# Attention and an MLP mixer on one core: order settings by 32 score tiles, a second buffer for the MLP's inner layer, and a last inversion between block transposes

## The chip, the core and the metric

One Trainium2 chip, one core. The metric is the device time of one execution in microseconds.

## The reference

A gate mixes a 32-head attention block with a shifting MLP; all inputs are bf16, S = 2048, D = 512, F = 1792.

```python
def _A_ref(x, wqkv, wo):                       # 32 heads of 16
    q, k, v = split_heads(x @ wqkv)
    p = softmax(einsum("bhqd,bhkd->bhqk", q, k) * 16 ** -0.5)
    return merge_heads(einsum("bhqk,bhkd->bhqd", p, v)) @ wo

def _B_ref(x, w1, w2, w3, w4):
    h = gelu(layernorm(x) @ w1)
    hs = shift_quarters_along_S(h) @ w2        # by +1, -1, +2, -2
    x1 = x + hs
    return x1 + gelu(layernorm(x1) @ w3) @ w4  # w3: 512x1792

g = sigmoid((x * gate_w).sum(-1, keepdims=True))
return g * _A_ref(x, ...) + (1 - g) * _B_ref(x, ...)
```

## The kernel before

The attention is done in 32 rounds (4 chunks of 512 queries, 4 groups of 8 heads, 2 halves). A round has 64 score tiles: 4 heads, each with 16 blocks of 128 keys against 512 queries. In all there are 2048 tiles. TensorE makes scores in its row mode (contraction over 32 rows, four heads one below the other) and everything else, the products with V ("PV") and all projections, in its column mode. A tile's exponential goes one of two ways:

- ScalarE takes two tiles in one 1024-wide exponential (buffers PA).
- VectorE takes one tile by a trick on the bits of the number, then adds three constant shifts to a pair of tiles (buffers PD). Two shifts run on VectorE, the third usually on GpSimd. All four versions are multiplied by V and summed on TensorE.

What makes this kernel unusual is that the order of its instructions comes from a list scheduler inside the kernel. It carries a duration for each operation, plays the engines forward when the kernel is built, and emits the instructions in the order in which they started. I call what it computes the plan. Its constants decide what TensorE takes next:

```python
    DVE_STOP = 6        # VectorE takes no more tiles when so few are left in a round
    AHEAD = 9           # how early the next round may begin
    FILL = 250          # how long TensorE idles before it multiplies zeros
    SL = (45, 60)       # slack in the budget of column work
    # ... some twenty more, one value each for the whole kernel
    P_W3 = ((740, 900), (975, 1250), (1314, 1520), (1719, 1830))   # first layer of the inner MLP, by tile
    P_W4 = ((991, 903), (1260, 1330), (1560, 1640), (1850, 2008))  # second layer
    NPA, NPD, NW = 9, 16, 9                                         # buffers
    # ...
    def pe_pick():
        # 1. new scores for ScalarE and VectorE wherever a PSUM bank is free
        # ...
        # 2. otherwise column work, as much as fits until the next bank comes free
        tr = min((j.start + j.hold + j.lat for j in exps if ...), default=None)
        budget = tr - t + SL[turn[0]] if tr is not None else IDLE_NS
        n = min(int(budget // 216.0), MAXU)
        g = gen_ready()                # a projection or an MLP product that is due
        # ... do_gen() and do_pv() in an order set by the constants
        if not ops:
            return filler(tr)          # matmuls of zeros
```

The GpSimd shift, the one inner-layer buffer and the product at the end of a round:

```python
    # close_pair, third shift of a pair of VectorE tiles (w = 1024):
    nc.gpsimd.tensor_scalar(out=d[k][:, 0:w], in0=d[0 if both else 2][:, 0:w], scalar1=1.0,
                            scalar2=float(SHIFT * (k if both else 1)), op0=ALU.mult, op1=ALU.add)
    # ... mlp2: all four chunks use hT
    h2 = hT[:].rearrange("p k s -> p (k s)")[:, 0:FT * 512].rearrange("p (f t) -> p f t", f=FT)
    # ... finish_round
    n = gp(1250, d3, lambda: nc.gpsimd.tensor_tensor(out=ob.slot[:], in0=ab.slot[:], in1=bb.slot[:], op=ALU.mult), ...)
```

The end of the kernel, where the last round's sums are inverted through TensorE:

```python
    nc.scalar.copy(out=ab[:], in_=acc[:])
    known(2); known(3)                                  # products that don't need the last round
    for b in range(4):                                  # the sums come onto partitions
        nc.tensor.matmul(pd[:, 4 * b:4 * b + 4], lhsT=ab[:, b * P:(b + 1) * P], rhs=idf[:, 0:P:32], ...)
    add_y(1)
    nc.vector.reciprocal(out=rdl[:], in_=pd.rearrange("p (b j) -> p b j", j=4))
    nc.vector.tensor_tensor(out=rdl[:], in0=rdl[:], in1=zE[...], op=ALU.mult)
    for b in range(4):                                  # and are spread again
        for j in range(4):
            nc.tensor.matmul(bc[32 * j:32 * j + 32, b * P:(b + 1) * P], lhsT=rdl[:, b, j:j + 1].to_broadcast([P, 32]), ...)
    add_y(3)
    for h in range(2):
        nc.vector.tensor_tensor(out=oT[...], in0=ab[...], in1=bc[...], op=ALU.mult)
```

The softmax here doesn't subtract the row's maximum and nothing guards it: scores larger than these inputs give would overflow.

## Time and profile before

| | before |
|---|---|
| median of 3 runs (lowest to highest) | 794.11 us (792.35 to 794.57) |
| span of the profiled execution | 790.1 us |
| PE, DVE, ACT busy | 98%, 95%, 94% |
| exponentials on ScalarE, tiles on VectorE | 736, 577 |
| matmuls of zeros | 300 |

Most lines are shown in the prediction. This is the timeline of TensorE in the kernel before: start in us, length in us, engine and line, operation, output and inputs, shapes, count.

```profile
7.50 1.05 PE L506 MATMUL ring<-w,w 128*32 128x512 bf16 x16
8.37 1.04 PE L506 MATMUL ring<-w,wq 128*32 128x512 bf16 x16
...
10.64 0.40 PE L812 MATMUL psA<-q,kT 32*128 32x512 bf16 x4
```

The first K projection runs at 7.50, and the first scores at 10.64.

A ledger of ScalarE is the measure used below. From the starts of all exponentials in the trace:

span = first exponential + pairs of neighbours x 0.903 us + what the pairs lose beyond 0.903 + other work (the GELUs) + from the last exponential to the end.

For the kernel before it reads 11.1 + 658.3 (729 pairs) + 57.9 + 51.0 + 11.8 = 790.1 us. The 57.9 is the room the change is after.

### The profile page before, as it was taken

The page shows a single profiled execution, that of the slowest core. Times are in us where ns is not written, and L with a number is a line of the kernel's source. Part 1 is how long each engine was busy: PE and PEld are TensorE (multiplying, and loading weights), DVE is VectorE, ACT ScalarE, POOL GpSimd, SP SyncE. Part 2 cuts the span into 40 slices and gives each one's busy share as a digit, 9 for nine tenths or more (in the row PEclk, how much of TensorE's full clock was granted, in tenths as well). Part 3 has the DMA queues.
Part 4 walks back from the last instruction along what each step waited for, and adds up shares of the span by engine and source line. Part 5 has one row for each costly group of instructions (what it writes and reads, how often), then busy time and mean ns, then how long its engine had stood idle before and what let it go on. Part 6 is the DMA issues. An engine that isn't in the chain of part 4 may idle for free.

```text
span 790.1 us, 24272 instructions
## 1 busy us (share of the span) xinstructions
PE 771.3 (98%) x9849; PEld 232.9 (29%) x9849; DVE 749.7 (95%) x1598; ACT 740.2 (94%) x762; POOL 343.8 (44%) x337
## 2 busy tenths in 40 slices
PE   8999999999899999999999999999999999999997
PEld 4333332222322222233222223222223222222223
DVE  6999999999999999999989999899999999999985
ACT  6999999999999999999989999999999999999995
POOL 3334343545444444453444434444444444444541
PEclk9999999999999999999999999999999999999999
DMA  9321302231000112143100011011000000000001
GB/s 210 116 57 54 80 7 73 44 92 66 20 3 20 51 39 57 33 114 104 30 24 22 20 26 39 29 27 37 22 19 19 23 27 29 11 20 19 17 19 32
DMA packets 64984, 34.63 MB, mean 44 GB/s; under 512 B 44636, under 2 KB 60268, under 8 KB 64872
## 3 DMA queue, kind: packets, MB, share of 16 engines
q1 hardware_dynamic: 63400, 32.42, 16.0%
q8 instruction: 77, 1.26, 0.7%
q10 hardware_dynamic: 1472, 0.66, 0.3%
q14 instruction: 35, 0.29, 0.1%
HBM read 17.39 MB, written 6.81 MB: 31 GB/s over the span
## 4 chain that ended last, share of the span: by engine, by line
PE 64%; DVE 26%; ACT 4%; issue 3%; DMA 1%; SPq 0%; POOL 0%; DVEq 0%; POOLq 0%; ACTq 0%
PE acc L988 22%; PE ring L506 20%; PE psA L812 20%; DVE PD L918 11%; DVE PD L954 8%; ACT PA L892 3%; DVE st L645 1%; PE ring L812 1%; DVE xn L665 1%; DVE hT L735 1%; DVE x_sb L714 1%; ACT hT L736 1%; DMA x_sb<-in_A_x_dram 1%; DVE accsb L1004 1%; DVE q L577 0%
## 5 line engine op out<-in xcount | busy, mean ns | idle before, releaser
L892 ACT ACTIVATE PA<-psA 128x1024 bf16<-128x1024 f32 x736 | 689.5, 1039 | 35.4 <-PE psA L812 18.4
L957 POOL TENSOR_SCALAR PD<-PD 128x1024 uint16<-128x1024 uint16 x275 | 289.4, 1053 | 412.1 <-DVE PD L954 291.2
L918 DVE TENSOR_SCALAR PD<-ring 128x512 uint16<-128x512 f32 x577 | 376.5, 679 | 12.4 <-PE ring L812 10.8
L988 PE MATMUL acc<-PD,V 128*17 128x512 bf16 x2308 | 308.9, 381 | 3.1 <-DVE PD L954 2.5
L812 PE MATMUL psA<-q,kT 32*128 32x512 bf16 x1471 | 279.1, 384 | 1.2 <-ACT PA L892 0.9
L988 PE MATMUL acc<-PA,V 128*17 128x512 bf16 x1471 | 268.3, 381 | 1.7 <-DVE accsb L1004 1.7
L954 DVE TENSOR_SCALAR PD<-PD 128x1024 uint16<-128x1024 uint16 (+1 forms) x592 | 240.9, 448 | 2.7
L812 PE MATMUL ring<-q,kT 32*128 32x512 bf16 x577 | 188.8, 383 | 1.3 <-DVE PD L918 1.2
L812 PEld LDWEIGHTS <-kT 32*128 32x128 bf16 x2048 | 72.6, 91 | 299.0 <-issue 298.1
L988 PEld LDWEIGHTS <-V 128*17 128x17 bf16 x3779 | 78.3, 88 | 142.1 <-issue 117.6
L506 PE MATMUL ring<-xnT,w 128*32 128x512 bf16 x1152 | 95.1, 383 | 2.3 <-DVE PD L918 2.2
L506 PE MATMUL ring<-w,hT 128*32 128x512 bf16 x1152 | 92.8, 383 | 1.8 <-DVE PD L918 0.8
L506 PEld LDWEIGHTS <-w 128*32 128x32 bf16 x1920 | 43.8, 95 | 49.8 <-issue 37.0
L1021 POOL TENSOR_TENSOR oT<-accsb,bcs 128x512 bf16<-128x512 f32 x31 | 40.4, 1305 | 8.5 <-DMA bcs<-rr 7.2
L506 PE MATMUL ring<-w,w 128*32 128x256 bf16 (+1 forms) x768 | 40.8, 311 | 0.5 <-DVE PD L918 0.4
L735 DVE CAST hT<-ring 128x512 bf16<-128x512 f32 x56 | 37.8, 678 | 0.9 <-PE ring L506 0.8
L506 PEld LDWEIGHTS <-hT 128*32 128x32 bf16 x1152 | 25.1, 95 | 36.0 <-issue 27.3
L1004 DVE COPY accsb<-acc 128x512 f32<-128x512 f32 x31 | 21.1, 681 | 4.7 <-PE acc L988 4.1
L736 ACT ACTIVATE hT<-hT 128x7168 bf16<-128x7168 bf16 x4 | 24.7, 6178 | 0.0
L645 DVE BATCH_NORM_STATS2 st<-x_sb 128x6 f32<-128x512 bf16 x32 | 21.6, 679 | 0.0
L1242 PE MATMUL acc<-zero 128*17 128x384 bf16 x300 | 20.6, 327 | 0.0
L506 PE MATMUL ring<-w,wq 128*32 128x512 bf16 x256 | 19.9, 382 | 0.0
(92 smaller groups left out, 233.8 us busy)
## 6 DMA issues: line engine op xcount, KB each, us to landing
bcs<-rr SPq DMA_DIRECT2D x124, 64.0 KB
xn_dram<-xn SPq DMA_DIRECT2D x32, 128.0 KB
w<-in_B_w_dram SPq DMA_DIRECT2D x5, 512.0 KB
oD<-oT SPq DMA_DIRECT2D x124, 16.0 KB
w<-in_B_w_dram SPq DMA_DIRECT2D x4, 448.0 KB
out_dram<-ot SPq DMA_DIRECT2D x14, 128.0 KB
x_sb<-in_A_x_dram SPq DMA_DIRECT2D x3, 512.0 KB
w<-in_A_wqkv_dram SPq DMA_DIRECT2D x2, 256.0 KB
```

The lines of the kernel that those rows point to most:

```text
L506: units.append([Op("col", j, lambda j=j, lf=lf, rf=rf, n0=n0, n1=n1, st=st, sp=sp: nc.tensor.matmul(get()[32 * j:32 * j + 32, n0:n1], lhsT ...
L645: a = dve(600, deps, lambda: nc.vector.bn_stats(out=sb.slot[:], in_=x_sb[:, t, :]), prio=6, at=at, acq=[sb])
L735: pre.append(evac(g, PSUM_NS, lambda ps, m=m: nc.vector.tensor_copy(out=h2[:, m, :], in_=ps[:])))
L736: ge = act(93 + 427 * FT + 2600, pre, lambda: nc.scalar.activation(out=h2, in_=h2, func=ACT.Gelu_apprx_tanh), prio=0)
L812: o = Op("row", i, lambda: nc.tensor.matmul(dst(), lhsT=kT[G][32 * i:32 * i + 32, kt * P:(kt + 1) * P], rhs=qbuf[G, c].slot[32 * i:32 * i ...
L892: job = act(hold, ops, lambda: nc.scalar.activation(out=pb.slot[:, 0:n], in_=buf.slot[:, 0:n], func=ACT.Exp, scale=0.25), acq=[pb], frees= ...
L918: nc.vector.tensor_scalar(out=pr["buf"].slot[:, h * 512:(h + 1) * 512], in0=buf.slot[:], scalar1=BITS_MUL, scalar2=BITS_ADD, op0=ALU.mult, ...
L954: nc.vector.tensor_scalar(out=d[k][:, 0:w], in0=d[0][:, 0:w], scalar1=float(SHIFT * k), scalar2=None, op0=ALU.add)
L957: nc.gpsimd.tensor_scalar(out=d[k][:, 0:w], in0=d[0 if both else 2][:, 0:w], scalar1=1.0, scalar2=float(SHIFT * (k if both else 1)), op0=A ...
L988: o = Op("col", i, lambda: nc.tensor.matmul(acc[32 * i:32 * i + DH + 1, :], lhsT=lhs(), rhs=rhs(), start=st, stop=True, tile_position=(0, ...
L1004: e = dve(PSUM_NS, round_ops[r], lambda: nc.vector.tensor_copy(out=ab.slot[:], in_=acc[:]), acq=[ab], prio=0)
L1021: n = gp(1250, d3, lambda: nc.gpsimd.tensor_tensor(out=ob.slot[:], in0=ab.slot[:], in1=bb.slot[:], op=ALU.mult), acq=[ob], frees=[ab, bb], ...
```

## The change

Its intent: give each stretch of 32 score tiles its own settings of the order; let two chunks of the inner layer overlap; invert the last round on VectorE alone. The core of the diff, with cuts marked:

```diff
-    DVE_STOP = 6
-    AHEAD = 9
-    ... (and some twenty more constants)
-    P_W3 = (..., (1719, 1830))
-    P_W4 = (..., (1560, 1640), (1850, 2008))
+    P_W3 = (..., (1525, 1830))
+    P_W4 = (..., (1560, 1715), (1850, 2008))
+    T1_DUE = 8
+    BASE = dict(P1_PRIO=0.414, DVE_STOP=6, DVE_STOP_L=8, AHEAD=9, IDLE_NS=537, ...)
+    SEG = 32
+    STAGES = {0: {'DUE_SH': -20, 'AHEAD': 7, 'GP2': 0.35}, 2: {'S_PRIO': 0.324}, ... , 64: {...}}
+    K = SimpleNamespace(**BASE)
-    NPA, NPD, NW = 9, 16, 9
+    NPA, NPD, NW = 8, 12, 9
+    hB = const.tile([P, FT * 512], BF16, name="hB")
+    h_of = {0: hT[...][:, 0:FT * 512], 1: hB[:]}
-        "xn": slots("xn", 4, [P, D]),
+        "xn": slots("xn", 2, [P, D]),
-        "big": [hT],
+        "big": [0, 1],
-        "bcs": slots("bcs", 2, [P, 512], F32),
+        "bcs": slots("bcs", 1, [P, 512], F32),
 ... first x transposes: blocks paired 0 and 2, 1 and 3
-        ks = (2 * half, 2 * half + 1)
+        ks = (half, half + 2)
 ... first Q projection (the first K projection keeps due=-3)
-                ... due=at + QDUE - QAT if at >= 0 else -1)
+                ... due=at + QDUE - QAT if at >= 0 else -4)
 ... pe_pick
+        if sim.tiles // SEG != stage[0]:
+            stage[0] = sim.tiles // SEG
+            K.__dict__.update({**BASE, **STAGES.get(stage[0], {})})
 ... the end
-    nc.scalar.copy(out=ab[:], in_=acc[:])
-    ... the two sets of matmuls through TensorE
+    nc.vector.transpose(out=tr[0][:], in_=acc[:])
+    nc.vector.reciprocal(out=rdl[:], in_=by32(tr[0])[:, :, 0])
+    nc.vector.tensor_tensor(out=rdl[:], in0=rdl[:], in1=zL[:], op=ALU.mult)
+    nc.vector.transpose(out=by32(tr[1]), in_=rdl[:].unsqueeze(2).to_broadcast([P, NT, 32]))
```

## The prediction

> **What bounds the kernel now.** I read the page's totals first, then the chain, the groups, the waits of ScalarE, and last the timeline at three places.
>
> ```profile
> span 790.1 us, 24272 instructions
> PE 771.3 (98%) x9849; PEld 232.9 (29%) x9849; DVE 749.7 (95%) x1598; ACT 740.2 (94%) x762; POOL 343.8 (44%) x337
> ...
> PE 64%; DVE 26%; ACT 4%; issue 3%; DMA 1%; SPq 0%; POOL 0%; DVEq 0%; POOLq 0%; ACTq 0%
> ...
> L892 ACT ACTIVATE PA<-psA 128x1024 bf16<-128x1024 f32 x736 | 689.5, 1039 | 35.4 <-PE psA L812 18.4
> L957 POOL TENSOR_SCALAR PD<-PD 128x1024 uint16<-128x1024 uint16 x275 | 289.4, 1053 | 412.1 <-DVE PD L954 291.2
> L918 DVE TENSOR_SCALAR PD<-ring 128x512 uint16<-128x512 f32 x577 | 376.5, 679 | 12.4 <-PE ring L812 10.8
> ...
> L1242 PE MATMUL acc<-zero 128*17 128x384 bf16 x300 | 20.6, 327 | 0.0
> ```
>
> Three engines are loaded nearly alike, and the chain hops between them: no single one is "the" bound. Busy time flatters them (a busy PE may be draining, a busy DVE may be held by GpSimd), so I counted in the trace records what each needs at its own shortest pace.
> - ScalarE: neighbouring exponentials start at best 0.903 us apart. 736 of them and the five GELUs with their table loads need about 714 us.
> - VectorE: starts at their usual distance (0.60 us for a tile read from PSUM, 0.335 us for a 1024-wide shift) add up to 709 us.
> - TensorE: 727 stretches of score matmuls lie between stretches of column matmuls. A cycle with up to 8 column matmuls takes 0.865 us, one with up to 12 takes 1.082: so 0.217 us per four, and 0.43 for the score part with its two changes of mode. 727 x 0.43 + some 1,800 fours x 0.217 = 704 us.
>
> All three can run only between the first exponential (11.1 us) and the end of the last scores (779 us): 768 us. Each therefore has 55 to 65 us of room, and 735 us (714 + 11 + 10) is where a perfect order would end. The time is set by the static order of instructions, not by an operation. Where is the room lost? Neighbouring exponentials (729 pairs) lose 58 us against 0.903 each: 28 us in 25 gaps over 1.6 us, some 8 us in 18 gaps of 1.2 to 1.6, and 21 us in many small ones, of which the 1.082 us cycles are a part.
>
> ```profile
> ACT PA L892 <- PE psA L812: 18.4, 19, 1.9
> ACT PA L892 <- PE ring L812: 9.9, 18, 1.5
> ACT PA L892 <- PE acc L988: 4.6, 12, 1.0
> ```
> ```profile
> 662.56 0.69 DVE L1004 COPY accsb<-acc 128x512 f32<-128x512 f32 x1 [0.20 <-PE acc L988]
> 662.88 0.11 PEld L812 LDWEIGHTS <-kT 32*128 32x128 bf16 x6 [0.42 <-issue]
> 662.89 0.39 PE L812 MATMUL psA<-q,kT 32*128 32x512 bf16 x4
> 663.12 0.38 PE L812 MATMUL ring<-q,kT 32*128 32x512 bf16 x2
> 663.28 0.53 SPq L1007 DMA_DIRECT2D den<-accsb  x1
> 663.38 1.94 ACT L892 ACTIVATE PA<-psA 128x1024 bf16<-128x1024 f32 x2 [0.82 <-PE psA L812]
> ```
>
> The waits are few and long, all for scores. The second view shows a typical one: a round of 64 tiles ends, TensorE finishes that round's products first, the accumulator is copied out, and the next scores come late. 31 such ends and 25 long gaps fit together. The other loss is at the five GELUs: there is no exponential for 8.7 us, and TensorE runs out of real work and multiplies zeros (300 matmuls; four side by side take 0.165 us, so 12 us).
>
> **What the Trainium skill says.** "TensorEngine Tiling (Array Packing)", section Key Properties: a change of tiling mode drains the array. The trace agrees: a score group issues in 0.22 us, yet costs 0.43 a cycle. So an order that needs fewer score stretches, or fills the columns between them, saves real time. "ScalarE: Activation LUTs", section What ACT_TABLE_LOAD costs, gives about 1283 ns for a load, plus about 1380 ns of drain; the trace has 1283 ns, but the load at 351.72 us starts where the exponential from 350.65 ends, so no such drain is seen. Neither load nor GELU is removed. "VectorE: DVE Perf Modes", section The three transpose paths: VectorE transposes 32x32 blocks only. That is all that the new ending needs; no transpose by VectorE is in this trace.
>
> **The change, part by part.**
>
> *The end.* The last round's inversion now runs as:
> ```profile
> 780.49 0.58 ACT L1279 COPY accsb<-acc 128x512 f32<-128x512 f32 x1 [1.54 <-PE acc L988]
> ...
> 781.20 1.06 PE L1283 MATMUL psA<-idf,accsb 128*128 128x4 f32 x8
> ...
> 782.36 0.26 DVE L1285 RECIPROCAL rdl<-psA 128x16 f32<-128x16 f32 x1 [4.44 <-PE psA L1283]
> 782.65 0.17 DVE L1286 TENSOR_TENSOR rdl<-rdl,zE 128x16 f32<-128x16 f32 x1
> ...
> 783.07 1.06 PE L1289 MATMUL psA<-idf,rdl 128*32 128x128 f32 x32
> ...
> 784.25 0.75 DVE L1293 TENSOR_TENSOR oT<-accsb,psA 128x256 bf16<-128x256 f32 x2 [1.42 <-PE psA L1289]
> ```
> From the copy to the final product 3.76 us, with a crossing between engines at each step. After: transpose out of PSUM, reciprocal, product with the gate, transpose of the broadcast, all on VectorE, which is idle there. I take 0.68 us for each transpose (what a 128x512 fp32 copy takes), 0.26 and 0.17 for the small ones: 1.8 us. The known products run on TensorE meanwhile. Gain 1.9 us, all on the path.
>
> *The start.* The first x transposes put column blocks 0 and 1 in one bank, one copied by ScalarE, one by VectorE, and VectorE waited for ScalarE there twice (the view of waits: 4.7 us in all, 3.6 the longer). Blocks are now paired 0 and 2, 1 and 3, one engine to a bank: the copies, which end at 6.67 us, end perhaps 0.4 us sooner. The second chunk's transposes (6.50 to 7.57) need no longer precede the first K projection at 7.50. Together 0.8 us.
>
> *Settings by 32 tiles.* Every second boundary of a stage is near the end of a round. The keys changed most (when VectorE stops taking tiles, how far ahead the next round is begun, urgency, tie rotation) act on just those ends. The earlier constants were one compromise for 31 ends; now each may have its own. I expect somewhat under half of the 28 + 8 us in long gaps, in part given back elsewhere: 11 us net. Of the 21 us in small gaps, 2 us. The shift of work between VectorE and GpSimd is a wash: the fractions add up to about 13 shifts moved to GpSimd and 14 moved back, of 0.335 us.
>
> *Second buffer for the inner layer.* Today the next chunk's first layer cannot start until the second layer of the present one has let go of the buffer; the plan shows it (third chunk's second layer ends at tile 1640, fourth chunk's first layer starts at 1719). With two, the fourth chunk starts at 1525 and this work can lie under a GELU. This reaches the windows at 351, 474 and 596 us, while 203 and 719 depend on the settings alone. Zeros worth 12 us, of which maybe half become useful fours, each worth at most 0.18 us (1.082 - 0.903) where it leaves a full cycle: 3 us.
>
> *What pays for it.* Exponential buffers 9 to 8, VectorE buffers 16 to 12, pairs in flight 5 to 3. Reconstructing occupancy from the trace (written, less last read): over 12 VectorE buffers are in use for 7 us of the span, all 9 exponential buffers for 2 us, 8 for 72 us. So the loss is small, 1 us. The four loads of the gate's 4-byte elements lie early, on a queue with room.
>
> Sum: 1.9 + 0.8 + 11 + 2 + 3 - 1 = 17.7 us; 794.1 - 17.7 = 776.
>
> **The rivals.** (1) The settings are fitted to the kernel's own timing of its engines, and the chip doesn't follow it. For: engines wait in places where a consistent plan would have none, and 26 shifts last over 0.56 us against a median of 0.42, held by GpSimd for some 19 us in all. Against: the chip keeps the order, and small errors are absorbed at the next wait. It would leave only the ends and part of the buffer: 785 to 790. (2) The shallower buffers bind at round ends, where products wait longest: GpSimd's chain of shifts would throttle VectorE with three pairs. It would cost 5 to 10 us: 782 to 790. (3) Three engines share the room so evenly that closing gaps on one exposes another; TensorE's 704 us plus partly filled fours then stop it: about 780. (4) A search with this many settings found far more, say half of the room on every engine: 762 to 768.
>
> **Range and chances.** Ends and start are nearly sure (2.7 us), the rest is between a fifth and over half of the 58 us. I predict 776 us, 763 to 787 in 8 of 10. The line for 2% is 778.2, just above my figure, so: faster 0.58, within 2% 0.41, slower 0.01.
>
> **What would show it.** Right: long waits of ScalarE for scores fall from 33 us to about 20; gaps over 1.6 us from 25 to about 15; fewer than 200 matmuls of zeros; from the last product to the final multiplication under 2 us; first exponential before 10.6 us; busy sums of ScalarE and VectorE hardly changed while the span falls. Wrong: the waits keep their size and only move; GpSimd or the VectorE buffers appear as what TensorE waits for; the count of score stretches rises over 727; or the new transposes take over 1 us each.

## The result, and the profile after

The changed kernel took 787.54 us (median of 4 runs, 786.39 to 789.32), against 794.17 for the kernel before in the same rounds. A ratio in this document is the mean time of one kernel's runs over the mean of the other's of the same rounds, so it is not quite the ratio of the medians that I quote. Here it is 0.9923, with a 95% interval of 0.9899 to 0.9947: about 6 us faster, where I had forecast 18; it counts as within 2%, to which I had given 0.41. Two later repeats (below) gave 0.9956 and 0.9947, so the mean of three is 0.9942, or 4.6 us.

One warning about the pair of traces: the profiled execution of the changed kernel is its slowest of four (789.32), the one of the kernel before its quickest (791.92). So I use the two repeats' traces as well.

The page of the changed kernel, the lines that answer to those shown of before:

```profile
span 787.5 us, 23893 instructions
...
PE 766.7 (97%) x9672; PEld 227.1 (29%) x9672; DVE 744.9 (95%) x1587; ACT 743.3 (94%) x764; POOL 339.2 (43%) x331
...
PE 57%; DVE 23%; ACT 12%; issue 3%; DMA 3%; SPq 1%; POOL 0%; ACTq 0%; POOLq 0%; DVEq 0%
...
L909 ACT ACTIVATE PA<-psA 128x1024 bf16<-128x1024 f32 x739 | 693.4, 1040 | 25.0 <-PE acc L1005 8.7
L974 POOL TENSOR_SCALAR PD<-PD 128x1024 uint16<-128x1024 uint16 x269 | 283.8, 1058 | 418.2 <-DVE PD L971 263.0
```

The three engines are as loaded as before, and the chain still hops between them. Only the shares moved: more of the chain lies on ScalarE (4 to 12%). There are three more exponentials (739) and seven fewer VectorE tiles (577 to 570). The waits of ScalarE for TensorE (us in all, times, longest in us):

```profile
ACT PA L909 <- PE acc L1005: 8.7, 25, 1.1
ACT PA L909 <- PE ring L829: 7.2, 14, 1.2
ACT PA L909 <- PE psA L829: 6.6, 12, 1.5
```

In all they fell from 32.9 to 22.5 us, near the forecast of 20. But the kinds moved apart: those for scores (psA, ring) fell from 28.3 to 13.8 us, and those behind products with V (acc) rose from 4.6 us in 12 waits to 8.7 us in 25, and are now first. The prediction had read all three lines as waits for scores. The timeline of TensorE at the start of the changed kernel:

```profile
8.94 1.90 PE L519 MATMUL ring<-w,wq 128*32 128x512 bf16 x16 [2.33 <-DMA wq<-in_A_wqkv_dram]
10.62 1.92 PE L519 MATMUL ring<-w,w 128*32 128x512 bf16 x16
...
13.44 0.39 PE L829 MATMUL psA<-q,kT 32*128 32x512 bf16 x4
```

Q now comes before K. TensorE waits 2.33 us for Q's weights, and then both projections take 1.9 us where they took 1.05. The first scores come at 13.44 instead of 10.64. The view of busy time in a window gives the granted clock for this stretch (after the window: its length; busy us and count of PE, weight loads, VectorE, ScalarE and GpSimd; then the granted clock, the DMA share and GB/s):

```profile
8.94:12.47 3.53, 3.53 (x32) 1.07 (x32) 1.41 (x2) 0.00 (x0) 0.00 (x0) 1.00 0.98 265
```

The granted clock reads 1.00, although 32 matmuls took 3.53 us, about half of their usual pace. But the clock records of this trace begin only at 13.4 us. In the two later traces they cover this stretch; the third reads 0.59 there, with half speed from 7.7 to 11.2 us:

```profile
8.51:11.71 3.20, 3.20 (x34) 1.20 (x35) 1.25 (x2) 0.00 (x0) 0.00 (x0) 0.59 1.06 255
```

The end, from VectorE's timeline of the changed kernel:

```profile
779.05 0.72 DVE L1306 STREAM_TRANSPOSE accsb<-acc 128x512 f32<-128x512 f32 x1 [1.93 <-PE acc L1005]
779.80 0.25 DVE L1307 RECIPROCAL rdl<-accsb 128x16 f32<-128x16 f32 x1
780.09 0.17 DVE L1308 TENSOR_TENSOR rdl<-rdl,zL 128x16 f32<-128x16 f32 x1
780.36 0.71 DVE L1309 STREAM_TRANSPOSE accsb<-rdl 128x512 f32<-128x512 f32 x1
781.10 0.76 DVE L1319 TENSOR_TENSOR oT<-acc,accsb 128x256 bf16<-128x256 f32 x2
```

From the accumulator to the final product it is 2.05 us (779.05 to 781.10) where it was 3.76. The ledgers, with the mean of the three traces of the changed kernel:

| us | first exp. | pairs | lost beyond 0.903 | other | from last exp. | span |
|---|---|---|---|---|---|---|
| before | 11.1 | 658.3 (729) | 57.9 | 51.0 | 11.8 | 790.1 |
| after, first trace | 14.5 | 661.0 (732) | 50.0 | 51.2 | 10.8 | 787.5 |
| after, mean of 3 | 13.6 | 661.0 | 49.4 | 51.2 | 10.8 | 786.0 |

And what the pairs lose, by size of the distance between two starts:

| | over 1.6 us | 1.2 to 1.6 us | under 1.2 us | zeros |
|---|---|---|---|---|
| before | 25, losing 28.2 us | 19, losing 8.5 us | 21.3 us | 300 |
| after | 11 or 12, losing 11.2 to 12.6 us | 35 to 37, losing 15.2 to 15.7 us | 21.5 to 22.6 us | 184 |

(The prediction counted 18 medium ones before; one, of 1.201 us, lies on the edge.) So the long gaps went away by 16 us, more than I had forecast, and there are twice as many medium ones. This is what a medium gap looks like, in the timeline of the changed kernel's third trace:

```profile
749.75 1.94 ACT L909 ACTIVATE PA<-psA 128x1024 bf16<-128x1024 f32 x2
...
750.07 0.39 PE L829 MATMUL psA<-q,kT 32*128 32x512 bf16 x2
...
750.39 0.83 PE L519 MATMUL ring<-w,hT 128*32 128x512 bf16 x12
...
751.16 0.39 PE L829 MATMUL psA<-q,kT 32*128 32x512 bf16 x2
...
751.48 0.39 PE L1005 MATMUL acc<-PA,V 128*17 128x512 bf16 x2
...
751.97 1.02 ACT L909 ACTIVATE PA<-psA 128x1024 bf16<-128x1024 f32 x1 [0.28 <-PE acc L1005]
```

From one group of scores (750.07) to the next (751.16) it is 1.09 us, because 12 useful column matmuls lie between them. ScalarE could use scores every 0.903 us; it starts at 751.97, some 1.3 us after the second of the two before (750.65). The full cycle explains 0.19 of the 0.41 us that are lost. The rest is another wait: the scores end at 751.55, but the exponential starts only 0.10 us after the two products from 751.48 have ended (751.87), and the view names products (acc) as what it waited for. An exponential doesn't read the accumulator. What it can wait for there is a buffer (PA) that a product with V has still to read; the change left eight of them.

To count such waits, the kernels were built again to learn which buffer each exponential writes. Then the end of its scores in the trace was compared with the end of the last product that reads this buffer's old contents. If the product ends later, by over 0.04 us, it is a wait for a buffer. What neighbours lose beyond 0.903 us, with the number of pairs:

| | over 1.0 us apart, waiting for scores | over 1.0 us apart, waiting for a buffer | up to 1.0 us apart |
|---|---|---|---|
| before | 39.7 us (86) | 7.3 us (18) | 10.9 us |
| after, mean of 3 | 25.4 us (79 to 85) | 13.4 us (33) | 10.7 us |
| b_small (below: before, with the smaller pools) | 31.6 us (81) | 25.2 us (47) | 10.3 us |
| b_twobuf (below: the second buffer besides) | 26.6 us (73) | 22.2 us (45) | 10.4 us |

Of the medium gaps, 6 of 19 were waits for a buffer before and 18 or 19 of 35 to 37 after: 12 or 13 of the 16 to 18 that were added. The plan has the same: 19 waits for a buffer with 6.9 us before, 32 with 10.8 us after. Full cycles are a smaller part: those with 9 to 12 column matmuls went from 201 to 222, those with exactly 12 from 170 to 158. That TensorE makes no pause tells nothing here: 35 of the 37 medium gaps of the third trace have none over 0.33 us, but neither had 17 of the 19 medium and 22 of the 25 long ones before.

### The profile page after: what moved, and what is told of

The parts are those of the page before. It is cut to its first block, busy times and chain, and to the rows that moved or that the text cites. A ratio compares the mean times of both kernels' runs of the same rounds, so it can differ in the third digit from the quotient of the medians.

```text
span 787.5 us, 23893 instructions
## 1 busy us (share of the span) xinstructions
PE 766.7 (97%) x9672; PEld 227.1 (29%) x9672; DVE 744.9 (95%) x1587; ACT 743.3 (94%) x764; POOL 339.2 (43%) x331
## 4 chain that ended last, share of the span: by engine, by line
PE 57%; DVE 23%; ACT 12%; issue 3%; DMA 3%; SPq 1%; POOL 0%; ACTq 0%; POOLq 0%; DVEq 0%
PE acc L1005 20%; PE ring L519 18%; PE psA L829 18%; DVE PD L935 9%; ACT PA L909 9%; DVE PD L971 7%; DMA xn_dram<-xn 1%; PE ring L829 1%; DVE st L662 1%; DMA wq<-in_A_wqkv_dram 1%; DVE V L605 1%; ACT hT L722 1%; ACT hT L753 1%; ACT hB L753 1%; DVE hB L752 1%
## 5 line engine op out<-in xcount | busy, mean ns | idle before, releaser
L974 POOL TENSOR_SCALAR PD<-PD 128x1024 uint16<-128x1024 uint16 x269 | 283.8, 1058 | 418.2 <-DVE PD L971 263.0
L1005 PE MATMUL acc<-PD,V 128*17 128x512 bf16 x2280 | 302.3, 381 | 2.6 <-DVE accsb L1021 1.4
L829 PE MATMUL psA<-q,kT 32*128 32x512 bf16 x1478 | 284.7, 384 | 3.4 <-ACT PA L909 3.1
L971 DVE TENSOR_SCALAR PD<-PD 128x1024 uint16<-128x1024 uint16 x586 | 241.4, 453 | 3.5 <-PE acc L1005 1.7
L829 PE MATMUL ring<-q,kT 32*128 32x512 bf16 x570 | 195.4, 384 | 2.8 <-DVE PD L935 2.5
L519 PE MATMUL ring<-w,hT 128*32 128x512 bf16 x704 | 58.2, 383 | 0.2 <-DVE PD L935 0.2
L1038 POOL TENSOR_TENSOR oT<-accsb,bcs 128x512 bf16<-128x512 f32 x31 | 40.3, 1301 | 10.9 <-DMA bcs<-rr 7.5
L519 PE MATMUL ring<-w,hB 128*32 128x512 bf16 x448 | 35.1, 383 | 0.0
L519 PEld LDWEIGHTS <-hT 128*32 128x32 bf16 x704 | 14.7, 95 | 19.3 <-issue 14.7
L752 DVE CAST hB<-ring 128x512 bf16<-128x512 f32 x28 | 18.9, 680 | 0.8 <-PE ring L519 0.7
L752 DVE CAST hT<-ring 128x512 bf16<-128x512 f32 x28 | 19.0, 684 | 0.2 <-PE ring L519 0.2
```

Source lines behind the costliest of these rows:

```text
L519: units.append([Op("col", j, lambda j=j, lf=lf, rf=rf, n0=n0, n1=n1, st=st, sp=sp: nc.tensor.matmul(get()[32 * j:32 * j + 32, n0:n1], lhsT ...
L752: pre.append(evac(g, PSUM_NS, lambda ps, m=m: nc.vector.tensor_copy(out=h2()[:, m, :], in_=ps[:])))
L829: o = Op("row", i, lambda: nc.tensor.matmul(dst(), lhsT=kT[G][32 * i:32 * i + 32, kt * P:(kt + 1) * P], rhs=qbuf[G, c].slot[32 * i:32 * i ...
L971: nc.vector.tensor_scalar(out=d[k][:, 0:w], in0=d[0][:, 0:w], scalar1=float(SHIFT * k), scalar2=None, op0=ALU.add)
L1005: o = Op("col", i, lambda: nc.tensor.matmul(acc[32 * i:32 * i + DH + 1, :], lhsT=lhs(), rhs=rhs(), start=st, stop=True, tile_position=(0, ...
```

## The experiments

The theories at the start of this work, in short:

- **Full TensorE.** Closing long gaps packs useful columns into cycles that are then too long for ScalarE. This is rival 3 of the prediction. No run tried it.
- **Misfit.** The settings were fitted to the plan, and the chip falls behind the plan by more than before.
- **Pools.** The shallower buffers, which pay for the second inner-layer buffer, throttle somewhere.
- **Start.** Q before K costs what the new transposes gain.

All 18 runs of experiments. "This" and "before" are medians; the difference in us is (ratio - 1) x the median before.

| run | this / before | ratio [95%] | us |
|---|---|---|---|
| after_again | 786.87 / 791.15 | 0.9956 [0.9934, 0.9978] | -3.5 |
| after_third | 788.34 / 791.74 | 0.9947 [0.9932, 0.9963] | -4.2 |
| a_kswap | 786.03 / 792.61 | 0.9919 [0.9901, 0.9936] | -6.4 |
| a_kswap2 | 786.18 / 791.74 | 0.9925 [0.9912, 0.9939] | -5.9 |
| a_kswap3 | 785.57 / 792.62 | 0.9908 [0.9893, 0.9922] | -7.3 |
| b_newtail | 790.29 / 792.61 | 0.9967 [0.9948, 0.9986] | -2.6 |
| a_fill255 | 799.9 / 792.61 | 1.0091 [1.0069, 1.0113] | +7.2 |
| b_fill255 | 810.5 / 792.61 | 1.0235 [1.0207, 1.0262] | +18.6 |
| b_small | 806.12 / 791.15 | 1.0194 [1.0169, 1.0219] | +15.3 |
| b_twobuf | 794.25 / 791.15 | 1.0044 [1.0020, 1.0068] | +3.5 |
| a_onebuf | 794.88 / 791.15 | 1.0051 [1.0026, 1.0076] | +4.0 |
| a_poolshort (wrong result) | 777.88 / 791.74 | 0.9822 [0.9807, 0.9837] | -14.1 |
| b_poolshort (wrong result) | 784.19 / 791.74 | 0.9891 [0.9873, 0.9909] | -8.6 |
| a_split | 787.80 / 791.18 | 0.9952 [0.9932, 0.9972] | -3.8 |
| b_split | 792.05 / 791.18 | 1.0007 [0.9989, 1.0026] | +0.6 |
| a_split_both | 784.82 / 791.18 | 0.9915 [0.9899, 0.9931] | -6.7 |
| a_norm | 784.15 / 792.62 | 0.9892 [0.9879, 0.9905] | -8.6 |
| b_norm | 793.69 / 792.62 | 1.0013 [1.0001, 1.0026] | +1.0 |

Names with a_ are variants of the changed kernel, with b_ of the kernel before.

### The start: K before Q (a_kswap, a_kswap2, a_kswap3)

Only the 32 matmuls of the first two projections change places on TensorE, after the order is made. Everything else stays where it was.

```diff
+    first_k.extend(o.fn for o in g.ops)     # in the first K projection, and first_q alike
     sim.order.sort(key=lambda x: (x[0], x[1]))
+    ks = [e for e in sim.order if e[2] in first_k]
+    sim.order[:] = [e for e in sim.order if e[2] not in first_k]
+    n0 = min(n for n, e in enumerate(sim.order) if e[2] in first_q)
+    sim.order[n0:n0] = ks
```

> The changed kernel with one thing moved: the 16 matmuls of the first K projection stand ahead of those of the first Q projection, every other instruction keeps its place. Theory START (the new order lets TensorE wait for Q's weights at 8.94 us and then run its matmuls at half pace, and this lost time is never won back): first scores at about 10.8 us instead of 13.4, and the whole 2.5 to 3 us shorter, about 784.7. Rival SLACK (the slip at the start is absorbed by later waits): 787 to 788, within 0.5 us of the changed kernel.

TensorE's timeline of the first of the three:

```profile
6.82 1.05 PE L519 MATMUL ring<-w,w 128*32 128x512 bf16 x16 [1.14 <-DMA w<-in_A_wqkv_dram]
8.31 1.05 PE L519 MATMUL ring<-w,wq 128*32 128x512 bf16 x16 [0.44 <-DMA wq<-in_A_wqkv_dram]
...
10.21 0.40 PE L832 MATMUL psA<-q,kT 32*128 32x512 bf16 x4 [0.30 <-DVE q L583]
```

K's weights are there earlier than Q's, K runs at 6.82, TensorE's longest wait shrinks from 2.33 to 1.14 us, and both projections are back at 1.05 us. The wait of 2.0 to 2.7 us for Q's weights is gone in all six traces with K first. The half pace is not: in a_kswap2 and a_norm both projections took 1.9 us, after waits of at most 0.56 us.

How fast the first matmuls run differs from one execution to the next in every order: the first 16 transposes took 1.3 us in eight of the twenty traces and 2.0 us in twelve. So the first exponential is compared within these two kinds (mean start in us, number of traces):

| first transposes | old order | changed | K first |
|---|---|---|---|
| 1.3 us | 11.3 (3) | 13.2 (2) | 11.0 (3) |
| 2.0 us | 12.7 (5) | 14.1 (4) | 11.9 (3) |
| all | 12.15 (8) | 13.8 (6) | 11.45 (6) |

So the changed start costs 1.4 to 1.9 us (1.65 over all traces) instead of gaining 0.8. K first is 2.2 us earlier than that in both kinds, and 0.3 to 0.8 us earlier than the old order: the transposes were worth at most what I had said, and the order of Q and K, which I had passed over in the diff (its due went from -1 to -4, past K's -3), lost more than that. The Trainium skill, "TensorE: Matmul & The Clock Gate", section What's actually happening, has TensorE at half its clock by default and after at least one idle window of about 3.4 us. The half pace agrees in size (1.90 against 1.05 us, and the 0.59 of the third trace), but there TensorE had been without matmuls for only 2.73 us. What sets the half pace off in one execution and not in another is not shown by these runs.

> The changed kernel with the first K projection ahead of the first Q, once more, on the chip where the changed kernel runs too. First exponentials so far: 11.1 to 12.8 us in five traces with the old start, 13.1 to 14.5 in four with the new one, 10.9 with K first. Theory START: 2 to 3 us faster than the changed kernel of this call. SLACK: within 0.7 us of it.

> The changed kernel with K first, as the yardstick on this chip. From the two ratios so far, 0.9919 and 0.9925: 0.992 of the kernel before, 785.5 to 786.5.

The first gave 0.9919, hardly better than the changed kernel's first result (0.9923). In the same call it was 0.9925 beside 0.9947, or 1.7 us with intervals that just overlap, and 0.9908 in another: a mean of 0.9917 against 0.9942, or 2.0 us. With three each the times alone leave the size uncertain; it fits the 2.2 us of the traces.

### The changed kernel again (after_again, after_third)

No edit.

> The changed kernel as it is, for a second profile and more rounds beside the others. The first profile fell on a slow run of it (789.3 against a median of 787.5) and that of before on a quick one (791.9 against 794.2). Theory START: first scores again at about 13.4 us. If the start costs 3 us that are never won back, it is 2.5 to 3 us slower than the version with K first (ratio to before about 0.995 against 0.992); if the slip is absorbed, the same ratio, 0.992.

> The changed kernel as it is, for the comparison with K first on one chip and a third profile. From the two ratios so far (0.9923 and 0.9956): 0.994 of the kernel before, about 787.5.

Measured: 0.9956 and 0.9947. The first result (0.9923) lay on the lucky side, and its trace on the unlucky one. The gap counts hardly moved over the three traces, so the tables above don't rest on one execution.

### The end alone (b_newtail)

The kernel before with the new last round; the order ahead of it is kept, except that 21 matmuls of known products, which stood among the last products with V, now stand behind them. The four loads of the gate stand behind the existing ones.

```diff
-    nc.scalar.copy(out=ab[:], in_=acc[:])
-    ... inversion through TensorE
+    nc.vector.transpose(out=tr[0][:], in_=acc[:])
+    ... as in the change
```

> The kernel before with the new last round only (block transposes on VectorE), the order of everything ahead of it kept. The prediction's term says 1.9 us (792.3). The traces say: from the accumulator's release to the end 9.64 us before and 8.45 after, so 1.2 us (793.0). Rival: nothing, since the products of the known parts now stand ahead of the last ones on TensorE and the end waits for them: 794.2.

Measured: 0.9967, 2.6 us (1.1 to 4.1); from the last exponential to the end 9.8 us instead of 11.8. The forecast of 1.9 us was right in size, but in part by luck. The inversion itself gained 1.7 us (3.76 to 2.05). Behind it 0.7 was lost: VectorE's first step of the output starts 1.61 us after the final multiplication began, against 0.99 before. The known products of the last group stand ahead of the output products in TensorE's order; that they are what holds it is read from the trace and not tried by a run. And 0.9 was gained ahead of the inversion by the moved products, which I had not priced: the last product with V ends 1.20 us after the start of the last exponential, against 2.06. In the changed kernel the stretch is 10.8. Behind the inversion it is alike (1.63), but 25 products with V are left when the last exponential starts, where b_newtail has 9, and the last of them ends after 2.31 us. So the gain of 0.9 is not seen there.

### Is the plan's point fitted, and does the chip follow it? (a_fill255, b_fill255)

FILL is how long TensorE must be idle before it multiplies zeros. From 250 to 255 ns means nothing on the chip, but it sends the plan down another path.

```diff
-    FILL = 250
+    FILL = 255
```

> The changed kernel with one constant moved that hardly matters by itself: TensorE may fill with zeros after 255 ns of idleness instead of 250. The kernel's own plan of its engines then ends its last product 12.1 us later (770.3 instead of 758.2), since the fitted settings meet another order. Theory FIT (the settings were chosen for the plan's end, and a good part of what the plan gains by them is not there on the chip): the chip loses far less than 12 us, 788 to 794. Rival PLAN (the chip follows the plan at a fixed distance of 20 us): 799 to 801.

> The kernel before with the same constant moved, 250 to 255: the plan's last product is 10.6 us later (778.1 instead of 767.4). Theory FIT: the chip loses clearly less than the plan does, 796 to 802. Rival PLAN (fixed distance of 12 us): 804 to 806.

When it is built, the plan's last product moves from 758.2 to 770.3 us in the changed kernel (+12.1) and from 767.4 to 778.1 in the kernel before (+10.7). The chip went from 0.9942 to 1.0091 (some +11.8 us) and up by 18.6. The first is inside what was expected of a chip that follows the plan (799 to 801), the second above it (804 to 806). So a constant without meaning costs more than the whole change gains, in both kernels, and the chip follows the plan in direction; in size it was 1.0 and 1.7 times the plan here. The idea that fitted settings don't reach the chip at all falls.

The plan alone, computed at 13 to 16 harmless values of FILL (250 to 295; not run on the chip), gives for the last product: before, least 767.4, median 774.9; after, least 758.2, median 772.0. Both kernels ship with their best point. In the neighbourhood the changed structure is worth 3 us by the medians, with a wide spread (before 767.4 to 778.1, after 758.2 to 779.4); the rest of the plan's 9.2 us is the fitting of this one path.

### Pools and the second buffer (b_small, b_twobuf, a_onebuf)

```diff
 # b_small: the kernel before with the changed kernel's pools
-    NPA, NPD, NW = 9, 16, 9
+    NPA, NPD, NW = 8, 12, 9
 # ... xn 4 to 2, bcs 2 to 1
 # b_twobuf: b_small with the second inner-layer buffer and the new places in P_W3, P_W4
-        "big": [hT],
+        "big": [0, 1],
 # a_onebuf: the changed kernel with one buffer
-        "big": [0, 1],
+        "big": [0],
```

> The kernel before with only the smaller pools that pay for the second buffer (8 and 12 score buffers, 2 and 1 of the small ones). The prediction's term: 1 us slower, 795. The kernel's own plan says 10.7 us later (778.1 instead of 767.4). If the chip follows the plan as it did with the constant moved: 803 to 811.

> The kernel before with the smaller pools, the second buffer and the new places of the MLP's work, its settings as before. The prediction's terms: 2 us faster, 792. The plan says 1 us later (768.4), and over 16 variants of one harmless constant its median is 775.0 against 774.9 for the kernel before: the second buffer only pays for its own space. So 793 to 799 if the chip follows the plan; under 790 if the second buffer brings on the chip what the plan doesn't see.

> The changed kernel with the second buffer not used (settings, pools, places and all else as changed). The prediction's term: 3 us slower, 790.5. The plan says 14.1 us later (772.3), as it does for any change that breaks the fit of the settings to this order: its median over 15 variants of a harmless constant is 776.5 with one buffer and 772.0 with two, so the buffer itself is worth 4.5 us of plan. On the chip 799 to 804 if it follows the plan.

Measured: +15.3, +3.5 and +4.0 us against before. Taken at face value, the smaller pools cost 15 us, the second buffer brings back 12, and in the changed kernel it is worth 8.6 (+4.0 against -4.6). But the run before has just shown that leaving a fitted point costs 12 to 19 us by itself, and each of these leaves one: the zeros rise from 300 to 524 in b_small. The chip again goes the plan's way: the last product in the plan is 767.4, 778.1 and 768.4 us for before, b_small and b_twobuf (the differences are +10.7 and -9.7 us; the chip has +15.3 and -11.8), and 772.3 for a_onebuf (+14.1 over 758.2; the chip +8.6, below the 799 to 804 expected). The plan's medians over the values of FILL are the fairer measure: 774.9 before, 778.3 with small pools, 775.0 with the second buffer on top. So the pools cost 3.4 us in the neighbourhood and the second buffer pays them back, 3.3. A run of one point can't show this; it stays a statement about the plan. What the runs do show is where ScalarE waits with the smaller pools: behind products with V for 17.6 us in 30 waits in b_small and 15.3 in 33 in b_twobuf, against 4.6 in 12 before, and by the count of buffers 47 and 45 waits against 18. The shipped pools aren't the only cause: b_fill255, with nine exponential buffers, has 25 such waits that lose 21.5 us. But in all traces the kernels with nine have 18 to 25 of them, and those with eight 29 to 47. With one buffer the changed kernel's median is 776.5 (4.5 worse), and without the settings by stage 791.8 (793.9 at its shipped FILL): in the plan the new base values alone are worse than the old constants; they and the stages are fitted together.

### What GpSimd takes from VectorE (a_poolshort, b_poolshort)

The lag is the start of a group of scores on the chip less its start in the plan. In the changed kernel it grows from the first scores to the last by 16.0, 14.0 and 15.8 us (three traces), in the kernel before by 10.6, with the new end by 9.9. So of what the plan gains the chip loses 5.0 us (15.3 less 10.3) on the way. One suspect is GpSimd: a VectorE shift that usually takes 0.42 us lasts up to 1.5 us. The Trainium skill, "SBUF — State Buffer", section Who interferes with whom, says that GpSimd and a VectorE instruction in a two-port mode contend for one pair of ports as an exclusive lock, so that whoever starts first keeps it for the whole instruction. No view shows the mode of these shifts; that they get longer beside GpSimd's fits. To test it, GpSimd shifts only a quarter of its columns. The rest keeps old values, so these two kernels compute a wrong result. (The comparison with the reference doesn't see this.)

```diff
+    sim.emit(4200.0, lambda: [nc.gpsimd.memset(b[:].bitcast(F32), 0.0) for b in sim_pd])
-    nc.gpsimd.tensor_scalar(out=d[k][:, 0:w], in0=d[0 if both else 2][:, 0:w], ...
+    nc.gpsimd.tensor_scalar(out=d[k][:, 0:w // 4], in0=d[0 if both else 2][:, 0:w // 4], ...
```

> The changed kernel with GpSimd's shifts cut to a quarter of their columns (a wrong result on purpose; every instruction, wait and place is kept, the buffers are cleared once at the start). Theory CONTENTION (the chip falls behind the kernel's plan in the middle because GpSimd's shifts hold up VectorE's, and because this eats more of the tighter plan): the 14 to 16 us that this order falls behind between the first and the last score shrink to about 5, so 776 to 779, and the distance to the same cut in the kernel before is what the plan says, 9 to 11 us. Rival OTHER (TensorE's own pace, DMA or semaphores make the distance): 785 to 787, and the distance to the kernel before stays 4 to 6 us.

> The kernel before with GpSimd's shifts cut to a quarter in the same way (wrong on purpose). CONTENTION: the 10.6 us that this order falls behind shrink to about 4, so 785 to 788. OTHER: 792 to 793.

The groups of the quarter in the changed kernel (line, engine, operation, shapes, count, busy us and mean ns, idle before), then the full shift in its third trace:

```profile
L973 DVE TENSOR_SCALAR PD<-PD 128x1024 uint16<-128x1024 uint16 x586 | 227.1, 426 | 3.6 <-PE acc L1007 1.7
L976 POOL TENSOR_SCALAR PD<-PD 128x256 uint16<-128x256 uint16 x269 | 111.5, 418 | 554.2 <-DVE PD L973 344.6 <-PE ring L831 71.4 <-PE acc L1007 51.0
```
```profile
L971 DVE TENSOR_SCALAR PD<-PD 128x1024 uint16<-128x1024 uint16 x586 | 240.2, 449 | 3.5 <-PE acc L1005 1.7
```

VectorE's shifts lose 23 ns of their mean (449 to 426; 13 us of busy time), and those over 0.56 us lose 6.8 us instead of 18 to 20. The time falls by 9.9 us in the changed kernel (0.9822 against 0.9947) and by 8.6 in the kernel before. The lag's growth falls from 15.3 to 5.0 and from 10.3 to 1.8: by 10.3 and 8.5 us. So most of the lag in both kernels comes with GpSimd's shift, by its hold on VectorE or by its own lateness, and the difference between the two kernels, 1.8 us, explains a third of the 5.0. The other 3.2 are open. The theory CONTENTION expected the two cut kernels to lie 9 to 11 us apart; they lie 6.3 apart, nearer to its rival.

### Shorter instructions on GpSimd (a_split, b_split, a_split_both, a_norm, b_norm)

If the hold counts, two half-width instructions should free VectorE sooner. The a_ kernels here have K first.

```diff
 # a_split, b_split
-    nc.gpsimd.tensor_scalar(out=d[k][:, 0:w], ...
+    for a in range(0, w, w // 2):
+        nc.gpsimd.tensor_scalar(out=d[k][:, a:a + w // 2], ...
 # a_norm, b_norm (a_split_both has both)
-    n = gp(1250, d3, lambda: nc.gpsimd.tensor_tensor(out=ob.slot[:], ...
+    n = gp(1250, d3, lambda: [nc.gpsimd.tensor_tensor(out=ob.slot[:, a:a + 256], ...) for a in (0, 256)], ...
```

> The changed kernel with K first and every GpSimd shift issued as two instructions of half the columns (right results, order and waits kept, GpSimd has the time). Theory CONTENTION in its exact form (a VectorE shift that meets a GpSimd instruction waits until that one instruction is over): the excess of long shifts falls from 19 us to about 10, and the kernel gets 3 to 5 us faster than K first alone, 781 to 783 where the kernel before takes 792. Rival LATENESS (the cut to a quarter helped because GpSimd's results came sooner, not because it held VectorE): the halves end later, 1.2 us after the start instead of 1.05, so no gain or 1 to 3 us slower, 786 to 789.

> The kernel before with the same halved GpSimd shifts. CONTENTION: 2 to 4 us faster than before, 788 to 790. LATENESS: 792 to 794.

Halving the shifts gained nothing: 0.9952 where K first has 0.9917, and 1.0007 for the kernel before. Of what was expected this is LATENESS, not CONTENTION. A half takes 0.63 us where the whole takes 1.05, so two take longer, and VectorE's busy time in shifts rose from 240.2 us (the line above) to 245.7. VectorE's shifts over 1.2 us became fewer (8 instead of 17), those over 0.56 us more (34 instead of 24).

> As the first of this call, and GpSimd's 31 products of the rounds (1.3 us each) in two halves too. CONTENTION: another 0.5 to 1 us. LATENESS: no gain or slower.

> The changed kernel with K first and only GpSimd's 31 products of the rounds (1.3 us each, fp32) issued as two halves; the shifts stay whole. Halving both was 2.9 us faster than halving the shifts alone, and with it all VectorE shifts over 1 us vanished. Theory HOLD (a VectorE shift waits for the GpSimd instruction that it meets, and the longest, the products, do the harm): 2 to 3 us faster than K first alone in this call, 783 to 784. Rival CHANCE (the 2.9 us were the spread between runs and orders): within 1 us of K first alone.

> The kernel before with GpSimd's 31 products in two halves. HOLD: 1 to 3 us faster than before (789 to 791 where it takes 792). CHANCE: within 1 us.

With the round's product (1.3 us on GpSimd, 31 times) halved too, all VectorE shifts over 1.2 us are gone, and the kernel was 3.0 us faster than a_split. The product's halves alone gave 784.15 us against 785.57 for K first, with overlapping intervals (1.4 us, between HOLD's 2 to 3 and CHANCE's 1), and nothing in the kernel before (+1.0 us), where HOLD had 1 to 3 us of gain. So I can't say whether a hold of VectorE or the lateness of GpSimd's own results makes the 10 us of the quarter test. That is left open.

The best kernel with right results is thus the changed one with K first, 785.6 to 786.2 us; with the product's halves it had 784.15, which the intervals don't separate from it.

## Why the prediction was right or wrong

The forecast was 776 us; the measurement lies just above the top of my range. By its own steps, the time in us being the change against before:

| step of the sum | forecast | measured |
|---|---|---|
| the end | -1.9 | -2.0 alone (time -2.6); -1.0 in the changed kernel's traces |
| the start | -0.8 | +1.65; -0.3 to -0.8 with K first |
| settings by 32 tiles, small gaps and second buffer | -16 | -14.5: waits for scores -14.3, pairs up to 1.0 us apart -0.2 |
| shallower buffers | +1 | +6.1: waits for an exponential buffer |
| more exponentials on ScalarE | none | +2.7 (three more pairs) |
| sum | -17.7 | -5.0 with the lines above, and -4.6 for the mean of three |

- **The bound** was read rightly: three engines in balance, no operation at fault. The mechanism named for the settings, long waits at round ends, did shrink: of 25 long gaps 15 lay within 1 us of a copy of the accumulator, of the 11 or 12 after only 3. I had forecast 15 in all. (The ten others don't fit "31 such ends and 25 long gaps".)
- **The step that failed** is "what pays for it": "So the loss is small, 1 us". It measured 6.1 us: ScalarE's waits for an exponential buffer went from 18 to 33 and what they lose from 7.3 to 13.4 us. This is 5 of the 12.7 us missing. Two readings led there. I took the waits of ScalarE as "all for scores", though 4.6 us of them stood behind acc. And I found all nine buffers in use for 2 us only; counted from the start of the exponential that writes a buffer to the end of the last product that reads it, it is 40.7 us. It is my rival 2 (782 to 790) in another place: I had looked for it in GpSimd's chain and VectorE's buffers. That the ninth buffer makes the waits, and not the new order, is not isolated: no run gives the changed order a ninth.
- **The settings, small gaps and second buffer** together gained 14.5 of the 16 us forecast, as fewer and shorter waits for scores; these runs can't part them. The zeros fell from 300 to 184, within my line of 200.
- **Three more exponentials** on ScalarE cost 2.7 us at 0.903 each, which I had not counted, and **the end** kept 1.0 of its 1.9.
- **Rival 3**, closing gaps on one engine exposes another, holds in part: the limit met in the added medium gaps was most often a buffer and not TensorE's time. The 21 more cycles with 9 to 12 column matmuls are an estimated 3.8 us at most, at 0.18 us each (1.082 - 0.903).
- **The start** failed at a line of the diff that I did not cost: Q's due before K's. It is worth 2.4 us of the 12.7 missing.
- **Rival 1**, a chip that doesn't follow the plan, holds in a mild form. The plan itself gained 9.2 us at its last product, and 10.3 at its last scores; of this the chip loses 5.0 us in the middle by a lag that grows faster, and 2.5 at the start (the lag at the first scores is 3.7 us on average, 1.2 before). With the new end the plan held some 11 us. So a part of my 17.7 was never in the order at all, and I could have known only by reading what the order promised.
- **The list of signs** was met where it asked for waits (22.5 against "about 20"), zeros, and long gaps, and the time didn't follow. Its sign for the waits took all kinds together, and so hid that one kind grew. The end took 2.05 us where it asked for under 2. Two signs pointed the right way: the first exponential was not before 10.6 us, and the score stretches rose from 727 to 738, which I had listed as a sign of being wrong. I had priced one at 0.43 us of TensorE, so 11 of them are an estimated 4.7 us of its time; no run tried what they cost by themselves.

What stays open: how much of the waits for a buffer is the ninth buffer's loss and how much the new order, 3.2 us of the lag's growth, whether GpSimd's part in it is a hold or lateness, and what each of the some sixty groups of settings is worth, since none can be taken out without leaving the fitted path.

## What to carry to other kernels

When several engines are balanced, a long wait that is closed is not worth its length, because the next limit is near. Look at buffers too: here the waits of ScalarE that ended with a product it doesn't read were waits for a free buffer, and a buffer is in use from the start of its writing to the end of its last reading. An order fitted by search sits on a sharp point, so one-part experiments measure the loss of the fit first; compare neighbourhoods (here, a constant without meaning) before believing in a part's worth. And read every due and priority in the diff of a scheduler: swapping two projections moved the first exponential by 2.2 us, as much as the whole new ending gained alone (2.0).

## What the Trainium skill lacked or had wrong

- "TensorE: Matmul & The Clock Gate", section What's actually happening, ties the half clock to an idle window of about 3.4 us. In the third trace of the changed kernel 16 matmuls took 1.90 us instead of 1.05 after TensorE had been without matmuls for only 2.73 us (from 5.78 to 8.51), and the clock was half from 7.7 us, 2.0 us after the last matmul.
- "ScalarE: Activation LUTs", section What ACT_TABLE_LOAD costs: the drain of about 1380 ns beside the load is not seen; the load at 351.72 us starts where the exponential from 350.65 us (1.06 us long) ends, and the GELU starts at 353.02 us, where the load (1.28 us) ends.
- "SBUF — State Buffer", section Who interferes with whom, agrees in form with VectorE shifts of up to 1.5 us against 0.42. It doesn't say that shorter GpSimd instructions don't lessen the whole: with GpSimd's shifts in halves, VectorE's busy time in its own rose from 240.2 to 245.7 us.
- "GPSIMD Engine Reference" has no time for a multiply and add by constants on uint16. The runs show 1.05 us for 1024 columns, 0.63 for 512 and 0.42 for 256.
- "VectorE: DVE Perf Modes", section The three transpose paths, has a time for 128x128 bf16 only. A 128x512 fp32 transpose by 32x32 blocks took 0.72 us out of PSUM and 0.71 from a broadcast operand, much like the 0.68 of a copy.
